# When the planner of an attention and GeGLU kernel may put zero products on TensorE

## The chip, the cores and the metric

One core of one Trainium2 chip runs the whole program. The metric is the device time of one execution in microseconds (us). The kernel before has a median of 792.99 us over five runs (791.52 to 793.93). The profile that is read below is of one execution of 792.45 us; its span from the first to the last instruction is 790.7 us, so 1.75 us of that execution lie outside the span.

## The reference

One transformer block on x of 2048 rows by 640 columns in bf16: 32 query heads of width 20 share one key head and one value head, and a gated MLP of width 1536 follows.

```python
h  = x + attention(layernorm(x))      # q = n @ wq, k = n @ wk, v = n @ wv, one k and v for 32 heads
                                      # softmax(q k^T / sqrt(20)) v, all heads side by side, then @ wo
h2 = h + (gelu(n2 @ w_gate) * (n2 @ w_up)) @ w_down      # n2 = layernorm(h)
```

## The kernel before

The rows are cut into 16 tiles of 128. Query rows are worked in nine chunks (seven of two tiles, two of one), and within a chunk in units of 512 query columns for each of four heads at a time. For a unit, each of the 16 key tiles gives a **pack** (`issue_qk`, L1092, product at L1149): four score tiles of 128 keys x 512 queries, computed side by side on four row groups of TensorE, each into a PSUM bank of its own (banks 0 to 5, sometimes 6 and 7).

A score tile is made into weights in one of two ways. ScalarE takes the exponential (L1489, one tile or a pair of neighbouring banks). Or VectorE makes a 16-bit approximation (`dve_decide`, L1583), of which GpSimd writes two shifted copies (L1552); such a tile costs three value products later, an exact one costs one. How many tiles of a pack go to VectorE (`n` in L1100 to L1111) follows from the load that the planner sees on both engines at that moment, from the free banks and from `stall`.

The value products (`issue_pv`, L1228) use four column groups of TensorE, one block of four products for the four row groups of heads, and add up in an accumulator bank (6 or 7) until the unit is closed and copied out (L1255). Projections, the MLP's products and the output projection go piecewise between them (`issue_piece`, all through the helper line L548). In this text a **block** is four products side by side on the four row or column groups.

The order of work on all five engines is not written by hand. A planner in Python (the loop at the end, L1698) walks forward in its own time: it takes the engine that is free first, asks that engine's `..._decide` for an instruction, and commits it with an estimated cost and latency; where there is nothing, the engine's time moves on by 20 ns. `plan.resolve` then sets the semaphore waits. Each engine's program is the order so found, and the hardware runs it in that order. Costs in the plan: 216 ns for a block of 512 columns, plus up to `SW` = 105 ns where the mode of TensorE changes between scores (`"q"`) and column-group work (`"v"`), in `pe_sw`.

`pe_decide` (L1271) issues a pack if four banks are free, else a value block, else a piece of another job. If none of these is to be had before the next pack is expected (`fits`, against `lim`), and if `quiet(t)` holds, `fill(t)` (L1342) issues a block of **zero products**: a weight of zeros (`zz`) against the first 512 columns of the keys, added to the accumulator of an open unit, which leaves the sum as it is. `quiet` adds up the planned time of TensorE in the last 3400 ns and compares it with `QUIET`. `fill` asks for a unit whose four row groups have started and with over 8 value products still to come (`u["todo"]`), and for the first four key tiles.

The start of the program (the head) loads x, computes the first layer norm tile by tile on VectorE, transposes the normed tiles by DMA on SyncE's queue (L487), and makes keys and values (`kv_job`) as tiles arrive, while the first packs already run. The four large weight loads (L983) come on the same SyncE queue behind a gate of planned time (L984):

```python
sp_tasks.append(_Task(("sp",), (lambda o, v: lambda e: e.dma_start(o[:], cview(v)))(o, v), 1500, 12000,
                      [], [nm], 9.0, None, lambda: plan.free["sp"] > 30000.0))
```

The second layer norm of a chunk (L423 to L496) is also VectorE work, and stands among the packs of a later chunk.

Of the kernel before, what the change touches and what calls it, by code (L numbers as in the profile page):

```python
# [9 lines left out]
P = 128  # L10
# [194 lines left out]
def bass_sequential_preLN__grouped_kv_mqa__glu_gated_geglu__prompt_kernel(  # L205
# [53 lines left out]
    def sb(name, shape, dt):  # L259
        cm = nc.sbuf_tensor(name, shape, dt)  # L260
        t = cm.__enter__()
        allocs.append(cm)
        return t
# [13 lines left out]
    kT4 = sb("kT4", [P, S], BF16)  # L277
# [12 lines left out]
    zz = sb("zz", [P, 32], BF16)  # L290
# [14 lines left out]
    ps = ps_cm.__enter__()  # L305
# [9 lines left out]
    plan = _Plan()  # L315
# [23 lines left out]
    SP2G = (300.0, 300.0, 300.0)  # L339
    ADD_MIN = 1  # L340
    PVF = 99
    QUIET = 0.5
    PADD_DVE = 1
    PADD_LEN = (3, 3, 3)
    PRA = 3
# [14 lines left out]
    L_PE, L_ACT, L_DVE, L_POOL = 232.0, 310.0, 150.0, 100.0  # L360
# [625 lines left out]
    def pe_sw(t, mode):  # L986

        if mode == state["mode"] or not plan.ops["pe"]:
            return 0.0
        return max(0.0, plan.ops["pe"][-1].end + SW - t)  # L990
# [6 lines left out]
    def open_units():  # L997
        return [u for u in units if u["npk"] > 0 and not u["evac"]]
# [272 lines left out]
    def pe_decide(t):  # L1271
# [58 lines left out]
        if fits(222.0 + swv) and quiet(t):  # L1330
            return fill(t)
        return False

    def quiet(t):
        busy = 0.0
        for o in reversed(plan.ops["pe"]):
            if o.end < t - 3400.0:
                break
            busy += min(o.end, t) - max(o.t0, t - 3400.0)
        return busy < QUIET * 3400.0  # L1340

    def fill(t):  # L1342

        u = next((u for u in open_units() if u["acc"] is not None and all(u["started"]) and u["todo"] > 8), None)
        if u is None or not all(("k", k) in plan.w and plan.ready("pe", [("k", k)], ()) <= t for k in range(4)):
            return False
        ab = u["acc"]

        def fn(e):
            ins = None  # L1350
            for r in range(4):
                ins = e.matmul(ps[32 * r:32 * r + 32, ab * 512:(ab + 1) * 512], zz[:], kT4[:, 0:512], start=False,
                               stop=False, tile_position=(0, 32 * r))
            return ins
        sw = pe_sw(t, "v")
        state["mode"] = "v"
        plan.commit("pe", fn, 216.0 + sw, L_PE, ["zz"] + [("k", k) for k in range(4)], [("b", ab)], at=t)
        state["fills"] = state.get("fills", 0) + 1
        return True

# [337 lines left out]
    while True:  # L1698
        eng = min(order, key=lambda e: plan.free[e])
        t = plan.free[eng]  # L1700
# [4 lines left out]
        if eng in ("pe", "dve", "act"):  # L1705
# [10 lines left out]
            k = (int(t // 100000), eng, why)  # L1716
# [23 lines left out]
    n = 0  # L1740
# [63 lines left out]
```

## Time and profile before

| what | value |
|---|---|
| median of five runs | 792.99 us (791.52 to 793.93) |
| the profiled execution, its span | 792.45 us, 790.7 us |
| mean granted TensorE clock | 0.976 |
| ScalarE busy, whole span; 60 to 765 us | 731.8 us; 686.2 of 705 us |
| TensorE busy | 698.2 us |
| VectorE and GpSimd busy | 613.9 and 655.4 us |
| zero products (L1352) | 148, that is 37 blocks, first at 33.9 us, last at 697.7 us |
| score tiles by ScalarE | 593 alone (653 ns each), 417 pairs (1078 ns each) |
| score tiles by VectorE | 621 (688 ns each) |

The rows are of the profile's page and its groups by line and shape. "PE" is TensorE, "ACT" ScalarE, "DVE" VectorE, "POOL" GpSimd, "SP" SyncE. A product's time in the profile includes the way through the array, so four products side by side show about 0.38 us busy when alone; in an unbroken run a block of 512 columns comes every 0.22 us.

### The profile page before, as it was taken

Reading aid. Unit: us, or ns where it says so; the run is one execution under the profiler, and the core shown is the slowest. Engines: PE = TensorE matmul, PEld = TensorE weight load, DVE = VectorE, ACT = ScalarE, POOL = GpSimd, SP = SyncE. Lnnn points to the kernel's source line nnn. Section 1 sums busy time; section 2 is a strip of 40 time slices with the busy share of each in tenths; the row PEclk is TensorE's granted clock in tenths of the full one; section 3 lists DMA queues with packets and bytes.
Section 4 is the critical chain, followed back from the end, with each engine's and each line's share of the span. In section 5 each row is a group of like instructions: output and inputs, shape, how many; then the busy total and the mean of one; then the engine's idle time right before and its main releaser. Section 6 shows DMA issues by size and latency. Waiting matters only on the chain.

```text
span 790.7 us, 29325 instructions
## 1 busy us (share of the span) xinstructions
PE 698.2 (88%) x12863; PEld 329.9 (42%) x12863; DVE 613.9 (78%) x1096; ACT 731.8 (93%) x1057; POOL 655.4 (83%) x708
## 2 busy tenths in 40 slices
PE   5668788888889899999889899999998989989998
PEld 3323223332234444445233444445543444434457
DVE  7948878888787877877787877868779787877854
ACT  5769999999999999999999999999999899999981
POOL 5569989999978997898987988789888898988860
PEclk9989999999989999999998999999999999989999
DMA  6790001100100012100010001200021001110000
GB/s 195 143 300 8 8 8 25 26 9 9 25 17 17 2 18 35 26 26 9 8 26 18 10 10 34 35 19 9 11 42 26 9 2 18 35 25 17 12 19 18
DMA packets 56606, 25.85 MB, mean 33 GB/s; under 512 B 47648, under 2 KB 55200, under 8 KB 56480
## 3 DMA queue, kind: packets, MB, share of 16 engines
q1 hardware_dynamic: 55168, 23.55, 13.3%
q8 instruction: 102, 1.67, 0.9%
q10 hardware_dynamic: 1312, 0.44, 0.3%
q14 instruction: 24, 0.20, 0.1%
HBM read 10.21 MB, written 2.62 MB: 16 GB/s over the span
## 4 chain that ended last, share of the span: by engine, by line
PE 57%; ACT 20%; DVE 15%; POOL 3%; DMA 3%; issue 2%; POOLq 0%
PE ps L548 21%; PE ps L1228 17%; ACT pa L1489 16%; PE ps L1149 16%; DVE pd L1583 10%; PE ps L544 3%; ACT gbuf L888 3%; POOL pd L1552 2%; DVE osb L1255 1%; DMA xn1T<-xn_tmp 1%; ACT L1489 1%; ACT L888 1%; DMA xh<-in_A_x_dram 1%; DVE xn_tmp L496 1%; DVE qT L618 1%
## 5 line engine op out<-in xcount | busy, mean ns | idle before, releaser
L1489 ACT ACTIVATE pa<-ps 128x512 bf16<-128x512 f32 (+1 forms) x1010 | 686.6, 829 | 31.3 <-PE ps L1149 25.3
L1552 POOL TENSOR_TENSOR pd<-pd,shifts 128x512 int32<-128x512 int32 x569 | 580.5, 1039 | 85.2 <-DVE pd L1583 80.1
L1583 DVE TENSOR_SCALAR pd<-ps 128x512 uint16<-128x512 f32 x621 | 416.4, 688 | 139.5 <-PE ps L1149 130.7
L1228 PE MATMUL ps<-pd,v_ext 128*32 128x512 bf16 x1863 | 292.2, 392 | 17.4 <-DVE osb L1255 10.1
L1228 PE MATMUL ps<-pa,v_ext 128*32 128x512 bf16 x1427 | 265.5, 394 | 3.1 <-DVE pd L1583 1.0
L1149 PE MATMUL ps<-qT,kT 32*128 32x512 bf16 x2048 | 206.6, 391 | 48.5 <-DVE pd L1583 30.0
L1149 PEld LDWEIGHTS ps<-qT,kT 32*128 32x128 bf16 x2048 | 57.0, 91 | 215.8 <-DVE pd L1583 130.6
L1228 PEld LDWEIGHTS ps<-pd,v_ext 128*32 128x32 bf16 x1863 | 80.1, 95 | 80.1 <-issue 37.1
L1228 PEld LDWEIGHTS ps<-pa,v_ext 128*32 128x32 bf16 x1427 | 71.1, 96 | 46.1 <-issue 26.7
L548 PE MATMUL ps<-xn2T,wu_sb 128*32 128x256 bf16 x1680 | 66.1, 274 | 2.8 <-DVE gbuf L905 1.7
L548 PE MATMUL ps<-xn2T,wg_sb 128*32 128x256 bf16 (+1 forms) x1748 | 67.9, 273 | 0.3 <-DVE gbuf L861 0.2
L548 PE MATMUL ps<-wd_sb,gbuf 128*32 128x320 bf16 x1344 | 65.3, 301 | 0.0
L548 PEld LDWEIGHTS ps<-xn2T,wg_sb 128*32 128x32 bf16 x1748 | 43.2, 97 | 19.7 <-issue 11.4
L548 PE MATMUL ps<-xn1T,wq_pad 128*32 128x256 bf16 (+1 forms) x1440 | 50.4, 266 | 0.8 <-POOL wq_pad L971 0.6
L548 PEld LDWEIGHTS ps<-xn2T,wu_sb 128*32 128x32 bf16 x1680 | 42.6, 96 | 19.7 <-issue 9.1
L548 PEld LDWEIGHTS ps<-wd_sb,gbuf 128*32 128x32 bf16 x1344 | 34.0, 96 | 24.2 <-issue 11.1
L548 PEld LDWEIGHTS ps<-xn1T,wq_pad 128*32 128x32 bf16 x1440 | 33.6, 97 | 14.1 <-issue 7.7
L905 DVE TENSOR_TENSOR gbuf<-ps,gbuf 128x512 bf16<-128x512 f32 x48 | 32.8, 682 | 8.5 <-PE ps L544 6.4
L1538 POOL TENSOR_TENSOR pd<-pd,shifts 128x256 int32<-128x256 int32 x50 | 33.4, 684 | 0.4 <-DVE pd L1583 0.4
L426 DVE BATCH_NORM_STATS2 stats<-xh 128x6 f32<-128x320 bf16 x64 | 30.0, 477 | 1.5 <-DMA xh<-in_A_x_dram 1.2
L548 PE MATMUL ps<-wo_sb,onT 128*32 128x320 bf16 x600 | 28.7, 301 | 1.5 <-DMA onT<-onq 1.1
L861 DVE CAST gbuf<-ps 128x512 bf16<-128x512 f32 x42 | 28.8, 685 | 0.9 <-PE ps L548 0.6
(73 smaller groups left out, 333.3 us busy)
## 6 DMA issues: line engine op xcount, KB each, us to landing
out_dram<-xh SPq DMA_DIRECT2D x16, 160.0 KB, 1.8
xh<-in_A_x_dram SPq DMA_DIRECT2D x3, 640.0 KB, 6.3
wg_sb<-in_B_w_gate_dram SPq DMA_DIRECT2D x1, 1920.0 KB, 10.9
wu_sb<-in_B_w_up_dram SPq DMA_DIRECT2D x1, 1920.0 KB, 10.8
wd_sb<-in_B_w_down_dram SPq DMA_DIRECT2D x1, 1920.0 KB, 15.4
wo_sb<-in_A_wo_dram SPq DMA_DIRECT2D x1, 800.0 KB, 5.1
onr<-osb SPq DMA_TRANSPOSE x30, 2.4
gbuf<-in_A_wq_dram ACTq DMA_DIRECT2D x1, 400.0 KB, 4.7
```

The lines of the kernel that those rows point to most:

```text
L426: dve(lambda e: e.bn_stats(stats[:, ln, t, 6 * h:6 * h + 6], xh[:, t, h * HALF:(h + 1) * HALF]), 395, [key], [("st", ln, t, h)], prio, c)
L544: return e.matmul(o(b), l, r, start=st, stop=sp)
L548: ins = e.matmul(o(b)[a, :], l[:, a], r, start=st, stop=sp, tile_position=(0, 32 * j))
L861: dve(lambda e: e.tensor_copy(o, i), c_dve(n * k), [("b", bk)], ks, 1.0, fin)
L888: task(("act",), (lambda v: lambda e: e.activation(v, v, ACT.Gelu_apprx_tanh))(v), ("gelu", c_act(n * (f1 - f0))), L_ACT, ks, ks, 1.0, (la ...
L905: dve(lambda e: e.tensor_tensor(o, i, o, ALU.mult), c_dve(n * k), [("b", bk)] + ks, ks, 1.0, fin)
L1149: ins = e.matmul(bank(b), kT4[32 * r:32 * r + 32, kt * P:(kt + 1) * P], qT[32 * r:32 * r + 32, s, :], start=True, stop=True, tile_position ...
L1228: ins = e.matmul(ps[32 * r:32 * r + 32, ab * 512:(ab + 1) * 512], v_ext[:, it["kt"], it["w"], :], it["ap"], start=st, stop=(j in ends), ti ...
L1489: op = plan.commit("act", lambda e: e.activation(dst, src, ACT.Exp, scale=SM_SCALE), cost, L_ACT, [("b", b0 + i) for i in range(n)], [("pa ...
L1538: return e.tensor_tensor(pd32[:, w, h], pd32[:, 0, h], shifts[:, w - 1:w].to_broadcast([P, 256 * k]), ALU.add)
L1552: return e.tensor_tensor(pd32[:, 1:3, h], pd32[:, 0, h].unsqueeze(1).to_broadcast([P, 2, 256]), shifts[:].unsqueeze(2).to_broadcast([P, 2, ...
L1583: op = plan.commit("dve", lambda e: e.tensor_scalar(pd[:, 0, s * 512:(s + 1) * 512], bank(b), CH_A, CH_B, ALU.mult, ALU.add), c_dve(512), ...
```

## The change

Five edits, all in the planner. `QUIET` goes from 0.5 to 0.55. `quiet` no longer counts an instruction's whole planned time but at most 213 ns at its end, which leaves out the mode change. `fill` asks for over `FTODO` = 4 value products still to come instead of over 8. Where the first four key tiles are not all there, two are enough, and the zero products are then 256 columns wide. The planned cost of a zero block becomes `n * P / 2.4 + 3.0`: 216.3 ns for four tiles in place of 216.0, 109.7 ns for two. Since every later decision of the planner sees the times that come out of this, the order of work after the first differing block can differ on all engines.

```diff
-    QUIET = 0.5
+    QUIET = 0.55
+    FTODO = 4
...
     def quiet(t):
+
         busy = 0.0
         for o in reversed(plan.ops["pe"]):
             if o.end < t - 3400.0:
                 break
-            busy += min(o.end, t) - max(o.t0, t - 3400.0)
+            busy += max(min(o.end, t) - max(o.end - min(o.end - o.t0, 213.0), t - 3400.0), 0.0)
         return busy < QUIET * 3400.0
 
     def fill(t):
 
-        u = next((u for u in open_units() if u["acc"] is not None and all(u["started"]) and u["todo"] > 8), None)
-        if u is None or not all(("k", k) in plan.w and plan.ready("pe", [("k", k)], ()) <= t for k in range(4)):
+        u = next((u for u in open_units() if u["acc"] is not None and all(u["started"]) and u["todo"] > FTODO), None)
+        n = 4 if all(("k", k) in plan.w and plan.ready("pe", [("k", k)], ()) <= t for k in range(4)) else 2
+        if u is None or not all(("k", k) in plan.w and plan.ready("pe", [("k", k)], ()) <= t for k in range(n)):
             return False
         ab = u["acc"]
 
         def fn(e):
             ins = None
             for r in range(4):
-                ins = e.matmul(ps[32 * r:32 * r + 32, ab * 512:(ab + 1) * 512], zz[:], kT4[:, 0:512], start=False,
+                ins = e.matmul(ps[32 * r:32 * r + 32, ab * 512:ab * 512 + n * P], zz[:], kT4[:, 0:n * P], start=False,
                                stop=False, tile_position=(0, 32 * r))
             return ins
         sw = pe_sw(t, "v")
         state["mode"] = "v"
-        plan.commit("pe", fn, 216.0 + sw, L_PE, ["zz"] + [("k", k) for k in range(4)], [("b", ab)], at=t)
+        plan.commit("pe", fn, n * P / 2.4 + 3.0 + sw, L_PE, ["zz"] + [("k", k) for k in range(n)], [("b", ab)], at=t)
```

## The prediction

> **What bounds the kernel now.** I read the page's busy line and slices first, then tables by stretch (60 to 765 us; then the 3.41 us steps in which the granted clock moves), then the chain around the clock's drops, and last the rows of the zero products. The busy line and the clock's slices:
>
> ```profile
> PE 698.2 (88%) x12863; PEld 329.9 (42%) x12863; DVE 613.9 (78%) x1096; ACT 731.8 (93%) x1057; POOL 655.4 (83%) x708
> ...
> PEclk9989999999989999999998999999999999989999
> ```
>
> ScalarE is the fullest engine. By stretch (us; busy us and instructions of PE, PEld, DVE, ACT, POOL; granted clock; DMA):
>
> ```profile
> 0.00:60.00 60.00, 36.95 (x670) 18.22 (x674) 42.18 (x127) 39.17 (x57) 34.95 (x67) 0.91 0.79 210
> 60.00:765.00 705.00, 638.45 (x11880) 292.09 (x11868) 561.36 (x948) 686.19 (x992) 618.88 (x640) 0.98 0.09 18
> ```
>
> From 60 to 765 us ScalarE idles for 705 - 686.2 = 18.8 us: no change of TensorE's order can win more there without giving ScalarE less to do. The head has 20.8 us of idle ScalarE more. The clock falls to half in eight places, 37.5 us in all. Below, three steps that came just before a drop, two after which the clock stayed whole, and four of the half-clock stretches:
>
> ```profile
> 97.17:100.59 3.42, 1.86 (x22) 0.51 (x22) 3.26 (x5) 3.39 (x7) 3.17 (x4) 1.00 0.00 0
> 418.03:421.44 3.41, 1.92 (x28) 0.55 (x24) 2.70 (x4) 3.27 (x5) 1.69 (x3) 1.00 0.17 34
> 609.17:612.59 3.42, 1.53 (x20) 0.57 (x20) 2.83 (x6) 2.67 (x5) 2.21 (x3) 1.00 0.50 96
> ...
> 28.91:32.32 3.41, 2.04 (x56) 0.97 (x55) 3.20 (x13) 2.21 (x4) 3.08 (x6) 1.00 0.77 77
> 394.13:397.55 3.42, 2.20 (x28) 0.72 (x24) 2.99 (x6) 3.42 (x7) 3.08 (x4) 1.00 0.02 5
> ```
>
> ```profile
> 100.59:104.00 3.41, 3.41 (x32) 0.77 (x28) 1.66 (x3) 2.15 (x4) 2.42 (x3) 0.50 0.41 43
> 230.29:237.12 6.83, 6.50 (x56) 1.26 (x52) 6.03 (x11) 5.75 (x8) 5.11 (x6) 0.50 0.15 26
> 421.44:424.85 3.41, 3.41 (x23) 0.60 (x23) 1.98 (x3) 2.08 (x5) 2.95 (x4) 0.50 0.24 48
> 612.59:616.00 3.41, 3.41 (x40) 1.20 (x43) 1.53 (x3) 2.35 (x4) 2.89 (x3) 0.50 0.02 5
> ```
>
> The reader is to see two things. A step with at most 1.92 us of busy TensorE was followed by half clock; of those I looked at, the emptiest that was not had 2.04 us. And in a half-clock stretch TensorE is full (3.41 of 3.41 us) while ScalarE, full before, idles: there TensorE is the bound.
>
> What comes ahead of a drop in mid-kernel is a layer norm's small work on VectorE, which frees score banks late. The chain at one of them (start, length, what):
>
> ```profile
> 228.31 1.03 DVE ln_veb L442
> 229.34 0.60 DVE pd L1583
> 229.94 0.14 issue
> 230.08 0.47 PE ps L1149 x4
> ...
> 232.02 0.97 PE ps L1228 x8
> 232.99 0.55 PE ps L1149 x3
> 233.54 0.97 PE ps L1228 x8
> 234.51 0.55 PE ps L1149 x4
> 235.06 0.55 PE ps L1352 x3
> ```
>
> TensorE had just been idle for 1.15 us waiting for L1583. The old rule placed no zero block there: its 3400 ns still held dense work, mode changes counted in.
>
> **The change, part by part.**
>
> *More zero blocks.* Counting 213 ns a block instead of 216 plus up to 105 lowers the counted load: with four changes in 3400 ns by about 0.42/3.4 = 0.12; the new bound adds 0.05. So the rule now asks for a real product share under 0.55 where it asked for about 0.35 to 0.5. In the timeline of TensorE I counted about 210 gaps of over 0.22 us, 116 us in all. Those with a share under 0.55 behind them hold about 137 blocks; the plan's gaps are not the trace's, so I take 100 new ones (60 to 140) beside the 37, most in the head, at 60 to 120, 180 to 230 and 380 to 425 us.
>
> *What a zero block costs.* It stands in a gap, so its own 0.22 us cost nothing while the gap is there. If the banks come free earlier than planned, the pack behind it, with ScalarE and VectorE behind that, is late by up to one block and a mode change: 0.21 us (its warm row on the chain, 114.20 us) to 0.33 (with a mode change as on the chain, 0.33 us a pack against 0.22 a block). Of the 37 blocks, five are on the chain, but four of these at half clock. Of some 31 at full clock, one: 0.21/31 = 0.007 us each, so 100 cost 0.7 us. Ends: 0, where every one is covered, and 100 x 0.33 x 1/4 = 8 us if every fourth hits. I take 0.7, by the nearest row, which is the same instruction.
>
> *The six drops in mid-kernel* (100.6, 230.3, 414.6, 421.4, 612.6 and 697.9 us, 27.3 us). ScalarE is busy there for 2.15 + 5.75 + 2.70 + 2.08 + 2.35 + 6.02 = 21.05 us, so it idles for 6.3. At full clock it wouldn't be full either: around the chunk end at 300 to 340 us, without any drop, it idles for 2.45 of 40 us, 6%, which is 1.6 us of 27.3. What can be won is 6.3 - 1.6 = 4.7 us. Five of the six need one more block in the step before (1.68 to 1.92 us of busy TensorE; a block alone shows 0.38), the one at 612.6 (1.53) about two. Each of these steps has a gap of 0.56 us or more, and its share at its end is low enough for the new rule. I take five sixths: -3.9 us. Ends: 0 and -4.7.
>
> *A rule against this.* The row: the gap of the drop at 230.3 us was 1.15 us, and none of the six had 3.4 us without a product. The Trainium skill ("TensorE: Matmul & The Clock Gate", "HAM oscillation — how this bites in real kernels") says that only a gap of over about 3.4 us must be avoided to keep the clock. By that rule alone one drop of eight, that behind the 5.3 us gap before 47.9 us, would be there, and this term would be 0 and the time 793.7. The rows speak against it.
>
> *The head.* Zero blocks 256 wide can now come before 33.9 us, while two key tiles exist. The step at 22.08 us had 1.35 us of busy TensorE, so it needs 0.6 us more, three to five narrow blocks. The todo bound lets them stand only between a pack and its value block, where gaps of 0.4 to 0.6 us lie at 23.5 and 25.3. If it works, the 2.32 us of key and value products at 25.88 us take half: 1.2 us. I take 0 of it, since the chain then goes through VectorE's layer norm and the 9.52 us at 38.28 in which a normed tile's transpose lands late behind the weight loads. The drop at 46 us, behind that wait, stays: the plan doesn't know the wait, and puts no block into it. Ends: 0 and -1.2.
>
> *The cost formula, 216.3 for 216.0 ns:* nothing that a 20 ns step shows. *No wait is added:* the keys are long there, and the last write of an accumulator stays a value block.
>
> *The order after it.* This the trace of before can't price. From both sides: two ends are the rivals below, +4.9 and -4.9 us by the load order, and +5 by the tiles' split. I take 0, as nothing in the rows gives a sign.
>
> Sum: 792.45 - 3.9 + 0.7 + 0 = 789.25 us against the profiled execution. The median of the runs shown lies 0.54 above it: 789.8 us, 0.4% faster.
>
> **The rivals.**
>
> *The blocks don't land where the drops are.* The planner counts 320 ns for the norm that took 596 (L496), 80 ns for steps that took 423 and 348 (L438, L442), so in its time those gaps are shorter than in the trace, and a zero block plus mode change needs 0.33 us. For it: no block was placed in five of the six steps before, though TensorE was at 1.5 to 1.9 of 3.4 us. Against it: three gaps of 0.56 us in the step at 609.17 alone. Then the drops stay and the blocks cost 0 to 1: 793 us (791 to 795).
>
> *Slower: more score tiles fall to ScalarE.* `n` is decided pack by pack from the loads at that instant (L1100 to L1111), and every instant after the first new block shifts. Price: 0.54 us of ScalarE for a tile in a pair (1078/2), 0.65 alone, on an engine 97% full. Ten tiles more of ScalarE's 593 + 2 x 417 = 1427 are 5.4 us. It decides from six tiles on: 6 x 0.54 = 3.2 us eats the net gain. With 13 tiles and the sum above: 789.8 + 7.0 = 797 us (793 to 800). For it: 1427 against 621 rests on thresholds. Against: the shift may go the other way as easily.
>
> *The load order in the head.* Two of the four weight loads left ahead of the last two transposes (L487 at 36.51 us). A load of 1920 KB at the 407 GB/s of 39 to 43 us is 4.8 us. One load more ahead: 789.8 + 4.8 = 795 us. One less: 785.
>
> **How the numbers follow.** About 0.2% (1.6 us) is what a measurement of this kernel can tell from no change. The forecast, 789.8 with 786 to 792, gets 0.44 (0.41 faster, 0.03 same): the rows of the drops are clear, but the gain is 4 us and the order moves. Blocks that don't land: 0.18 (0.04 faster, 0.08 same, 0.06 slower). Tiles to ScalarE: 0.27, slower. The load order: 0.11 (0.04 faster, 0.07 slower). Together: faster 0.49, same 0.11, slower 0.40. The range goes from 784.5 (one load less) to 800 (the upper end of the tiles); a fifth at most is left outside.
>
> **What would show it.** Right: L1352 with 400 to 700 products, some before 33.9 us; half-clock stretches of 10 to 20 us in all instead of 37.5, of which 6.8 at 46 us stay; ScalarE's idle time from 60 to 765 us at 14 to 16 us instead of 18.8. Wrong: as many drops as before (first rival), ScalarE's tiles over 1433 (second), three or more weight loads ahead of the last L487 (third), or many zero blocks on the chain at full clock (the cost term).

## The result, and the profile after

The changed kernel is slower: 795.64 us median (792.65 to 797.51) against 792.91 for the kernel before in the runs beside it, a ratio of 1.0036 with a 95% interval of 1.0026 to 1.0046. The forecast was 789.8 us. The profiled execution of the changed kernel has a span of 793.8 us. Its lines have moved by one to three: L1149 is now L1150, L1228 L1229, L1352 L1355, L1489 L1492, L1583 L1586, L487 L488, L983 L984, L725 L726.

The busy line and the clock's slices of the page after:

```profile
PE 705.3 (89%) x13176; PEld 334.9 (42%) x13176; DVE 617.1 (78%) x1106; ACT 729.3 (92%) x1060; POOL 659.0 (83%) x713
...
PEclk9979999999999999999999999999999999999999
```

The two stretches (us; busy us and instructions of PE, PEld, DVE, ACT, POOL; granted clock; DMA share; GB/s), and below them two steps of 3.4 us, each with the half-clock stretch that follows it:

```profile
0.00:60.00 60.00, 34.16 (x650) 17.00 (x654) 38.15 (x122) 35.38 (x52) 31.83 (x64) 0.92 0.79 210
60.00:765.00 705.00, 645.21 (x12136) 296.63 (x12128) 566.95 (x961) 684.78 (x996) 622.74 (x645) 1.00 0.09 18
```

```profile
47.53:50.94 3.41, 0.00 (x0) 0.00 (x0) 0.00 (x0) 0.08 (x1) 0.15 (x1) 1.00 1.43 279
50.94:61.18 10.24, 7.14 (x73) 2.16 (x73) 3.20 (x6) 3.97 (x6) 4.51 (x6) 0.50 0.68 214
231.87:235.28 3.41, 1.77 (x24) 0.59 (x28) 3.38 (x7) 2.70 (x6) 2.54 (x4) 1.00 0.21 43
235.28:238.70 3.42, 3.42 (x32) 0.76 (x24) 2.22 (x6) 2.66 (x4) 2.37 (x4) 0.50 0.24 48
```

Two things are to be seen. From 60 to 765 us the clock is whole but for one step of 3.4 us, behind a step with 1.77 us of busy TensorE; the six drops of mid-kernel have become one. And the head has got worse: ScalarE works 35.4 of the first 60 us instead of 39.2, nothing at all runs on TensorE from 47.5 to 50.9 us, and 10.2 us at half clock follow instead of 6.8.

The head's wait is on SyncE's queue. What that queue issued (start, length, engine, line, kind), first before, then after:

```profile
34.37 0.59 SPq L983 DMA_DIRECT2D wo_sb<-in_A_wo_dram  x1
35.01 0.52 SPq L983 DMA_DIRECT2D wg_sb<-in_B_w_gate_dram  x1
36.51 5.48 SPq L487 DMA_TRANSPOSE xn1T<-xn_tmp  x2
42.04 0.77 SPq L983 DMA_DIRECT2D wu_sb<-in_B_w_up_dram  x1
```

```profile
35.38 0.58 SPq L984 DMA_DIRECT2D wo_sb<-in_A_wo_dram  x1
36.01 0.52 SPq L984 DMA_DIRECT2D wg_sb<-in_B_w_gate_dram  x1
36.57 0.53 SPq L984 DMA_DIRECT2D wu_sb<-in_B_w_up_dram  x1
37.84 10.86 SPq L488 DMA_TRANSPOSE xn1T<-xn_tmp  x2
```

The third weight load now goes out ahead of the last two transposes of the first layer norm, and these take 10.86 us on the queue instead of 5.48. The chain says the same: it waits for that transpose until 47.80 us before and until 53.16 after. Before, then after:

```profile
38.28 9.52 DMA xn1T<-xn_tmp
```

```profile
45.32 7.84 DMA xn1T<-xn_tmp
53.16 0.09 issue
53.25 1.26 PE ps L549 x15
```

The zero products, before and after, in the groups by line and shape:

```profile
L1352 PE MATMUL ps<-kT,zz 128*32 128x512 bf16 x148 | 14.9, 415 | 0.0
```

```profile
L1355 PE MATMUL ps<-kT,zz 128*32 128x512 bf16 x456 | 41.5, 396 | 0.0
```

114 blocks instead of 37, the first at 24.3 us, and none of them 256 wide: wherever the planner placed one, four key tiles were there.

### The profile page after: what moved, and what is told of

It is laid out like the page before. It is cut to its first block, busy times and chain, and to the rows that moved or that the text cites. A ratio compares the mean times of both kernels' runs of the same rounds, so it can differ in the third digit from the quotient of the medians.

```text
span 793.8 us, 29951 instructions
## 1 busy us (share of the span) xinstructions
PE 705.3 (89%) x13176; PEld 334.9 (42%) x13176; DVE 617.1 (78%) x1106; ACT 729.3 (92%) x1060; POOL 659.0 (83%) x713
## 4 chain that ended last, share of the span: by engine, by line
PE 59%; ACT 16%; DVE 16%; DMA 6%; issue 1%; POOL 1%
PE ps L549 22%; PE ps L1229 17%; PE ps L1150 16%; ACT pa L1492 14%; DVE pd L1586 9%; PE ps L545 3%; DMA onr<-osb 3%; DMA xn1T<-xn_tmp 2%; ACT gbuf L889 2%; DVE osb L1256 1%; PE ps L1355 1%; DVE xn_tmp L497 1%; DMA xh<-in_A_x_dram 1%; POOL pd L1555 1%; DVE qT L619 1%
## 5 line engine op out<-in xcount | busy, mean ns | idle before, releaser
L1492 ACT ACTIVATE pa<-ps 128x512 bf16<-128x512 f32 (+1 forms) x1011 | 683.4, 821 | 37.0 <-PE ps L1150 31.0
L1586 DVE TENSOR_SCALAR pd<-ps 128x512 uint16<-128x512 f32 x628 | 420.0, 688 | 130.1 <-PE ps L1150 120.5
L1229 PE MATMUL ps<-pd,v_ext 128*32 128x512 bf16 x1884 | 292.2, 385 | 17.8 <-DVE osb L1256 12.9
L1229 PE MATMUL ps<-pa,v_ext 128*32 128x512 bf16 x1420 | 257.0, 386 | 4.7 <-ACT pa L1492 2.3
L1150 PE MATMUL ps<-qT,kT 32*128 32x512 bf16 x2048 | 203.3, 385 | 37.5 <-DVE pd L1586 18.3
L1150 PEld LDWEIGHTS ps<-qT,kT 32*128 32x128 bf16 x2048 | 56.3, 91 | 204.3 <-DVE pd L1586 130.2
L1229 PEld LDWEIGHTS ps<-pd,v_ext 128*32 128x32 bf16 x1884 | 80.2, 95 | 77.5 <-issue 30.4
L1229 PEld LDWEIGHTS ps<-pa,v_ext 128*32 128x32 bf16 x1420 | 69.7, 95 | 45.0 <-issue 25.0
L1355 PE MATMUL ps<-kT,zz 128*32 128x512 bf16 x456 | 41.5, 396 | 0.0
L1541 POOL TENSOR_TENSOR pd<-pd,shifts 128x256 int32<-128x256 int32 x54 | 35.5, 674 | 0.6 <-DVE pd L1586 0.6
```

What stands on the lines that cost most here:

```text
L1150: ins = e.matmul(bank(b), kT4[32 * r:32 * r + 32, kt * P:(kt + 1) * P], qT[32 * r:32 * r + 32, s, :], start=True, stop=True, tile_position ...
L1355: ins = e.matmul(ps[32 * r:32 * r + 32, ab * 512:ab * 512 + n * P], zz[:], kT4[:, 0:n * P], start=False, stop=False, tile_position=(0, 32 ...
L1492: op = plan.commit("act", lambda e: e.activation(dst, src, ACT.Exp, scale=SM_SCALE), cost, L_ACT, [("b", b0 + i) for i in range(n)], [("pa ...
L1541: return e.tensor_tensor(pd32[:, w, h], pd32[:, 0, h], shifts[:, w - 1:w].to_broadcast([P, 256 * k]), ALU.add)
L1586: op = plan.commit("dve", lambda e: e.tensor_scalar(pd[:, 0, s * 512:(s + 1) * 512], bank(b), CH_A, CH_B, ALU.mult, ALU.add), c_dve(512), ...
```

## The experiments

Two theories stood against each other at first. A: the load order costs 4 to 5 us, and the rest of the change wins 1 to 2. B: the load order is nearly hidden, and the zero blocks on the chain cost the 3 us. A ratio is always that to the kernel before, measured again beside the runs in question. No edit touches the planner's decisions: each changes the finished order or what a zero block issues, so that every instruction not named stays in its place. In the first four, DMA issues are moved on SyncE's queue just before `plan.resolve()`.

**1. The changed kernel with the load order of before.**

```diff
+    spq = plan.ops["sp"]
+    late = [plan.w["wu"][0]]
+    for op in late:
+        spq.remove(op)
+    at = 1 + max(spq.index(plan.w[("xn1T", t)][0]) for t in range(2, NT))
+    spq[at:at] = late
     plan.resolve()
```

> The changed kernel with every engine's order as it is, except that on SyncE's queue the third weight load (w_up) goes behind the last two transposes of the first layer norm, as in the kernel before. Theory A, the load order: the 1920 KB ahead of those transposes cost 4 to 5 us of the changed kernel's 795.6, and the zero blocks and the rest of the new order won 1 to 2 us. Then this runs at 791 to 792 us, ratio to the kernel before 0.997 to 0.999. Theory B, the zero blocks on the chain: the load order is nearly hidden by ScalarE's slack later, and the zero blocks cost about 3 us net. Then this runs at 794.5 to 796, ratio 1.002 to 1.004.

Measured: 789.03 us, ratio 0.9953 (0.9928 to 0.9978). The one load, put back, moves the changed kernel from 1.0036 to 0.9953, 0.83% or 6.6 us (4.4 to 8.7 with both intervals). This is theory A, and faster than the 791 to 792 us that it gave. The chain now waits for the last transpose until 48.53 us, 4.6 us less:

```profile
43.17 5.36 DMA xn1T<-xn_tmp
```

**2. The kernel before with the load order of after.**

```diff
+    spq = plan.ops["sp"]
+    op = plan.w["wu"][0]
+    spq.remove(op)
+    spq.insert(1 + spq.index(plan.w["wg"][0]), op)
     plan.resolve()
```

> The kernel before with every engine's order as it is, except that the w_up load goes ahead of the last two transposes of the first layer norm, as in the changed kernel. Theory A: slower by 4 to 5 us, 797 to 798 us, ratio 1.005 to 1.006, and ScalarE busy in the first 60 us falls from 39.2 to about 35 us. Theory B: 793 to 794 us, ratio 1.000 to 1.001.

Measured: 796.76 us, ratio 1.0058 (1.0038 to 1.0077), 4.6 us slower (3.0 to 6.1); ScalarE works 35.0 of the first 60 us. The chain waits for the last transpose until 51.93 us, 4.1 us more than before:

```profile
44.10 7.83 DMA xn1T<-xn_tmp
```

The same move of one DMA issue makes either kernel slower, by 4.6 and by 6.6 us. Theory B falls.

Which edit of the change moved the load? The order that the planner writes for SyncE's queue with each edit alone shows it (the number of weight loads ahead of the last two transposes):

```
edit alone                         loads ahead
213 ns counted in quiet                 3
QUIET 0.55                              3
todo bound 4                            2
cost formula of the zero block          2
```

Either of the first two is enough. They change no cost of a load; they shift the order in the planner's own time at the moments, after 30 us of it, when SyncE asks what to send next.

**3 and 4. All four loads behind the last two transposes**, in both kernels: the edit of run 1 with `late = [plan.w[k][0] for k in ("wo", "wg", "wu", "wd")]`.

> The changed kernel with all four large weight loads behind the last two transposes of the first layer norm on SyncE's queue; all else in its order. Theory A: three loads of 4640 KB in all leave the wait in the head, so over 8 us go from it if nothing else is late next; what is next is VectorE's layer norm, so 6 to 8 us: 788 to 790 us, ratio 0.994 to 0.996. Theory B: 794 to 795 us.

> The kernel before with all four large weight loads behind the last two transposes of the first layer norm; all else in its order. Theory A: the wait of 5 to 6 us on those transposes goes, and with it the half-clock stretch at 46 us: 787 to 789 us, ratio 0.992 to 0.995. Beside the third kernel it gives the worth of the zero blocks and the new order without the head's wait: by theory A the changed kernel is the faster of these two by 1 to 2 us, by theory B the slower by 3. Theory B: 792 to 793.

Measured: 793.97 us, ratio 1.0010 (0.9996 to 1.0025), and 792.75 us, ratio 1.0003 (0.9987 to 1.0018). Theory A missed in both. The times are near those that theory B gave (794 to 795, and 792 to 793), but the 3 us that it put between the two kernels aren't there, and its reason isn't what the chain shows. The wait for the last transposes of the layer norm had gone, and another came in its place: the loads now stood ahead of the first unit's transpose of outputs. The chain's wait for it, the changed kernel first, the kernel before second:

```profile
55.54 9.62 DMA onr<-osb
```

```profile
54.61 8.35 DMA onr<-osb
```

ScalarE works 51.8 and 53.2 us from 60 to 120 us, against 58.2 in both kernels as they were. A queue's load has to stand somewhere; the gain was given back one wait later.

**5 and 6. No zero blocks.** Run 5 takes the changed kernel with the load order of before, run 6 the kernel before. `zero` is the list of what `fill` committed.

```diff
+    out_of = set(map(id, zero))
+    plan.ops["pe"] = [op for op in plan.ops["pe"] if id(op) not in out_of]
+    for i, op in enumerate(plan.ops["pe"]):
+        op.idx = i
     plan.resolve()
```

> The changed kernel with the load order of the kernel before (789.0 us), and all 114 blocks of zero products left out as the program is written; every other instruction stays in its place. Theory A1, the clock: the zero blocks won the 3.4 us against the kernel before; without them the clock falls in more places than the eight of the kernel before, and this runs at 793 to 797 us, ratio 1.000 to 1.006. Theory A2, the split: the 3.4 us came from the seven score tiles fewer on ScalarE (1420 instead of 1427, 0.54 us each, 3.8 us), and the zero blocks pay only for themselves; then this runs at 788 to 790 us, ratio 0.994 to 0.997, whatever the clock shows.

> The kernel before without its 37 blocks of zero products; every other instruction stays in its place. Theory A1: more drops of the clock, 794 to 797 us, ratio 1.002 to 1.006. Theory A2: 791.5 to 793 us, ratio 0.999 to 1.001.

Measured: 795.27 us, ratio 1.0040 (1.0018 to 1.0061), with 58.0 us at half clock ahead of the end; and 795.83 us, ratio 1.0055 (1.0035 to 1.0075), with 47.8 us. So the 114 blocks of the changed kernel are worth 1.0040 - 0.9953 = 0.87%, 6.9 us, and the 37 of the kernel before 0.55%, 4.4 us. Both runs go as theory A1 has it. Without any block the two orders are equal within their intervals, although ScalarE has 1420 score tiles in one and 1427 in the other: no worth of the split shows, and the 788 to 790 us that A2 gave for run 5 are far off.

**7. Zero blocks half as wide**, on the order of run 1: `ab * 512:ab * 512 + 2 * P` and `kT4[:, 0:2 * P]` in `fill`'s product.

> The changed kernel with the load order of the kernel before (789.0 us), its 114 blocks of zero products 256 columns wide instead of 512, all in their places. If what a zero block costs is the time in which a pack stands behind it (some 10 us of zero blocks lie on the changed kernel's chain), half of that comes back where the clock holds: 786 to 788 us, ratio 0.992 to 0.994. If half a block is too little to hold the clock, the drops come back and it runs at 790 to 793 us.

Measured: 789.31 us, ratio 0.9968 (0.9950 to 0.9987); 17.1 us at half clock, against 6.8 in run 1. The time lies between the two that were expected, with no gain over run 1 (0.9953) and no loss beyond the intervals: inconclusive on the price of a block.

**8. The loads spread.** w_o and w_gate behind the last two transposes, w_up behind the first unit's transpose of outputs, w_down behind the second's.

```diff
+    spq = plan.ops["sp"]
+    loads = [plan.w[k][0] for k in ("wo", "wg", "wu", "wd")]
+    for op in loads:
+        spq.remove(op)
+    at = 1 + max(spq.index(plan.w[("xn1T", t)][0]) for t in range(2, NT))
+    spq[at + 2:at + 2] = loads[3:]
+    spq[at + 1:at + 1] = loads[2:3]
+    spq[at:at] = loads[:2]
     plan.resolve()
```

> The changed kernel with the loads spread on SyncE's queue: w_o and w_gate behind the last two transposes of the first layer norm, w_up behind the first unit's transpose of outputs, w_down behind the second's. With all loads behind the last two transposes, that first unit's transpose waited 8 to 10 us, which ate the gain; here nothing should stand before it. Theory A: the wait of 5.4 us that the changed kernel with the order of before still had at 43 us goes, and nothing takes its place: 784 to 786 us, ratio 0.989 to 0.992. If the two loads ahead still hold the unit's transpose, 788 to 791.

Measured: 786.90 us, ratio 0.9939 (0.9913 to 0.9965), a little above the 784 to 786 of theory A. The queue now runs without a long transpose (the longest of these two kinds takes 2.8 us), and from 36 to 72 us the chain waits for none:

```profile
44.61 0.58 SPq L984 DMA_DIRECT2D wo_sb<-in_A_wo_dram  x1
45.24 0.52 SPq L984 DMA_DIRECT2D wg_sb<-in_B_w_gate_dram  x1
56.84 1.19 SPq L726 DMA_TRANSPOSE onr<-osb  x1
58.08 0.58 SPq L984 DMA_DIRECT2D wu_sb<-in_B_w_up_dram  x1
```

**9. The same in the kernel before.**

> The kernel before with the loads spread on SyncE's queue as in the run at 786.9 us (w_o and w_gate behind the last two transposes of the first layer norm, w_up and w_down behind the first and second unit's transposes of outputs); all else in its order. It stands beside that run as the kernel before beside the changed one, without a load in anybody's way. Theory A1, the clock: the 77 blocks more are worth 2.5 to 3.5 us there too, so 789 to 790.5 us, ratio 0.996 to 0.998. If the gain of spreading the loads depends on the changed order, 791 to 793 us.

Measured: 785.62 us, ratio 0.9923 (0.9899 to 0.9946). Theory A1 asked for 0.996 to 0.998 and missed: without a load in the way, the kernel before is as fast as the changed one.

**10 and 11. Which zero blocks pay, loads spread.** The edit of run 5 with the list cut at 50 us of planned time: first without the 17 blocks of the head, then with them alone.

> The changed kernel with the loads spread (786.9 us), without the 17 blocks of zero products of the first 52 us; the other 97 stay. Theory A1: the head has several drops without them, among them the long one that the order without any zero block showed at 31.6 us (17.1 us), but the head also waits for VectorE and for loads; 0.5 to 2.5 us slower than with them, 787.5 to 789.5 us, ratio 0.994 to 0.997. If the head's blocks are worth nothing: 786 to 787.5.

> The changed kernel with the loads spread (786.9 us), with only the 17 blocks of zero products of the first 52 us; the 97 later ones are left out. Theory A1: the drops of the middle come back, some ten of them; 4 to 6 us slower than with them, 790.5 to 793 us, ratio 0.998 to 1.001. If the later blocks pay only for themselves: 786 to 788.

Measured: 787.93 us, ratio 0.9939 (0.9917 to 0.9961), and 788.65 us, ratio 0.9954 (0.9937 to 0.9971). Both intervals overlap that of run 8 (0.9913 to 0.9965): beside it, neither group shows a worth of its own. Run 15 below comes back to this.

**12. Each zero block issued twice**, loads spread: `for r in (0, 1, 2, 3, 0, 1, 2, 3):` in `fill`.

> The changed kernel with the loads spread (786.9 us), each of its 114 blocks of zero products issued twice in its place, 114 blocks more. The clock is whole already, so this measures what a block costs. By the prediction's term, 0.007 us each: 0.8 us more, 787.7 us, ratio 0.995. By the blocks on the changed kernel's chain, some 10 us for 114: up to 10 us more, 792 to 797 us, ratio 1.000 to 1.006. Every fourth hit at 0.33 us, the prediction's upper end: 9 us.

Measured: 795.96 us, ratio 1.0057 (1.0037 to 1.0077). Against the 0.9939 and 0.9917 of the two runs without the doubling this is 1.18 to 1.40%, 9 to 11 us for 114 blocks, 0.08 to 0.10 us each, near the upper ends of the forecast. The chain's shares by line, run 8 and then this one (the list goes on to the right):

```profile
by line: PE ps L549 22.0%; PE ps L1229 16.1%; ACT pa L1492 15.6%; PE ps L1150 15.5%; DVE pd L1586 8.7%; PE ps L545 2.7%; ACT gbuf L889 2.2%; DMA onr<-osb 2.1%; issue 1.5%; DVE osb L1256 1.4%; PE ps L1355 1.2%; DVE xn_tmp L497 1.1%; POOL pd 
```

```profile
by line: PE ps L549 21.6%; PE ps L1229 18.6%; PE ps L1150 17.3%; DVE pd L1586 9.3%; ACT pa L1492 8.9%; PE ps L1355 5.0%; PE ps L545 2.6%; ACT gbuf L889 1.8%; DMA onr<-osb 1.6%; DVE osb L1256 1.6%; issue 1.6%; DVE xn_tmp L497 1.1%; DVE stats
```

The zero products (L1355) go from 1.2% to 5.0% of the chain, and ScalarE's exponentials from 15.6% to 8.9%: more blocks stand on the chain, and ScalarE, which waits for packs, idles for 22.9 us between the 64th and the last pack in place of 16.9. That fits second blocks that find no room in the gaps.

**13 to 16. Head or mid-kernel.** Left open was where run 1 had its gain, since runs 8 and 9 showed none. Theory H: in the head, where the blocks take away the half clock behind the wait. Theory M: in mid-kernel, as predicted. The edits are those of runs 10 and 11 on the load order of before, and runs 8 and 9 again, side by side on one chip.

> The changed kernel with the load order of the kernel before (789.0 us), without the 17 blocks of zero products of the first 52 us; the other 97 stay. Theory H, the head: the gain of 3.4 us comes from the head's blocks, which keep the clock behind the wait for the loads; without them 791 to 793 us, ratio 0.998 to 1.001. Theory M, mid-kernel as predicted: the gain comes from the later blocks and stays; 789 to 790 us, ratio 0.995 to 0.997.

> The changed kernel with the load order of the kernel before (789.0 us), with only the 17 blocks of zero products of the first 52 us. Theory H: the later blocks pay about for themselves, so 789 to 791 us, ratio 0.996 to 0.998. Theory M: 792 to 795 us, ratio 1.000 to 1.004.

> The changed kernel with the loads spread on SyncE's queue, once more, on the same chip as the next. Theory H: with the wait gone there is nothing in the head to win, and the later blocks cost what they save: equal to the next within 1 us, both at 785 to 787 us. Theory M: faster than the next by 2.5 to 3.5 us.

> The kernel before with the loads spread on SyncE's queue, once more, on the same chip as the run before it. Theory H: 785 to 787 us, equal to it within 1 us. Theory M: slower than it by 2.5 to 3.5 us.

Measured: without the head's blocks 789.56 us, ratio 0.9966 (0.9950 to 0.9982); with them alone 792.51 us, 0.9993 (0.9974 to 1.0012). Most of the gain on the load order of before comes with the later blocks, as M has it. With the loads spread: 785.77 us, 0.9917 (0.9897 to 0.9938), and 786.66 us, 0.9925 (0.9901 to 0.9949): equal, as H has it. So neither holds alone. Run 15 is the kernel of run 8 once more, and beside it run 11, without the later blocks (0.9954, 0.9937 to 0.9971), is slower by 0.37% with intervals that barely touch: a worth of the later blocks with the loads spread is not shown, but not excluded either.

The traces give the place, one execution each, by the start of the 64th and of the last pack (us):

```
                                 64th pack   last pack   between
before                             114.7       763.2      648.5
after, load order of before        111.7       759.4      647.7
before, load order of after        118.8       765.0      646.2
after                              118.7       765.7      647.0
before, all loads behind           115.4       763.8      648.4
after, all loads behind            117.4       761.8      644.4
before, loads spread (two)     109.7, 110.0  757.1, 755.8  647.4, 645.8
after, loads spread (two)      111.3, 111.0  756.5, 756.2  645.2, 645.2
```

At the same load order the changed kernel is ahead between the two packs by 0.8 us where two loads stand before the transposes, by 0.6 to 2.2 with the loads spread and by 4.0 with all four behind; with three loads ahead it is behind by 0.8. Two executions of one kernel differ there by 1.6. Up to the 64th pack it is 3.0 us ahead with two loads before the transposes, level with three, and 1.0 to 2.0 behind where none stands there: in run 8 the last transpose of the layer norm goes out at 43.4 us, in run 9 at 38.9. In the whole time the change is clear of noise only with two loads ahead, 0.47% faster. With three the ratios are 1.0036 and 1.0058, with all four behind 1.0010 and 1.0003, and with the loads spread they are equal, all with overlapping intervals. So what the zero blocks of the change are worth depends on the load order, and how the small gain divides stays open.

## Why the prediction was wrong

The step that failed is *the order after it*, which was set to 0. The third rival had the mechanism, the place and nearly the time: one load more ahead of the last two transposes, +4.8 us, 795 us. It had a chance of 0.07 as a slower case. What the kernel's text did show was that SyncE's queue sends loads wherever it finds nothing else after 30 us of planned time, between transposes of tiles that VectorE delivers just then; a small shift can cross a boundary of that kind, and two of the change's edits do so alone, so it deserved more than a tenth. The mechanism is shown from both sides (runs 1 and 2): one load moved is 6.6 us in the changed kernel and 4.6 in the kernel before, where the sum had 0.

The rival's price of 4.8 us is about what the last transpose is late by: 4.6 us in the changed kernel (53.16 us against 48.53 in run 1) and 4.1 in the kernel before (51.93 in run 2 against 47.80). Whether the 6.6 us of the whole time is really more than the 4.6 isn't settled, since their intervals overlap. The traces have one thing that goes that way: behind the wait the changed kernel has 10.2 us at half clock, and none in run 1, while the kernel before has 6.8 us there and 10.2 with the moved load.

*The drops in mid-kernel* (-3.9 us): the blocks landed and six drops became one, so the first rival falls, and the rule on steps held: the one drop left followed a step with 1.77 us, under the 1.92. The sum without the load, 789.8 us, stands beside 789.0 in run 1. But that is probably partly luck, as the next paragraph tells, and it holds for this load order alone: with the loads spread the same blocks show no gain (runs 8, 9, 15 and 16), which the term didn't foresee.

*What a zero block costs* was mis-sized by about ten: 0.007 us taken, 0.08 to 0.10 measured for a second block in the same place. For the first in its place that is more likely a bound from above, as the gap is emptier then; no run measures it. The nearest row, one warm block of 31 on the chain, was a poor one: on the chain of the changed kernel zero products make up 1.3% of 793.8 us, about 10 us, where the prediction had 0.7, though time on the chain isn't yet time lost. Runs 5 and 6 show only what the blocks are worth with their cost taken off: 4.4 us for the 37 old ones, 6.9 for all 114, so about 2.5 for the 77 new ones. If the new ones cost near 0.09 us each, 7 us in all, they must have won more than the 4.7 us that the prediction took to be there, and two errors stood against each other; no run separates the two.

*The reading of ScalarE's idle time* failed: 14 to 16 us was forecast for 60 to 765 us, and it is 20.2 after and 22.5 in run 1, which is faster. Some 2 us of the 22.5 come from the fixed stretch, as run 1 has its last pack before 760 us; between the 64th and the last pack ScalarE idles for 17.1 us before, 18.5 after and 19.2 in run 1. Two things stand behind it. ScalarE has less to do, 729.3 us in place of 731.8: nine tiles alone more and eight pairs fewer are -2.7 us at 0.653 and 1.078. And the new order has small waits in stretches that had been full: from 380 to 400 us it works 19.1 us where it had worked 19.8, from 180 to 222 us 40.7 where it had worked 41.7. Run 5, without any zero block, has 19.0 and 40.8 there, which speaks for the order as the cause and not for the blocks.

*The number of blocks* (100 new, 60 to 140) was 77. The count behind it was too high: 116 us of gaps are more than the 790.7 - 698.2 = 92.5 us in which TensorE idles at all by the busy line. *The narrow blocks*, taken as 0, were 0, since none was placed. *More tiles to ScalarE*, the second rival: they went the other way, to 1420, and runs 5 and 6 show no worth of it.

*The rule weighed* (the Trainium skill, "TensorE: Matmul & The Clock Gate", "HAM oscillation — how this bites in real kernels") reads "no PE-idle gaps >~3.4µs". Keeping to it is again not enough here: the step ahead of the drop at 235.28 us had 1.77 us of busy TensorE, so at most 1.64 us of gap. That shorter gaps are harmless, as the prediction read it, the sentence doesn't say.

## What to carry to other kernels

A planner that sends large loads on a queue "when nothing else is ready" can put them ahead of short transfers on which everything waits, and a small change elsewhere may move one across: compare the order of each DMA queue before reading anything else out of two traces. Such loads are placed by what comes behind them: all of them behind one critical transfer only held up the next, while spreading them, two behind the last transposes of the layer norm and one behind each of the next two transposes, gave the fastest versions here, 785.6 to 786.9 us, with either zero-block rule (ratios 0.9917 to 0.9939). Idle products that hold the clock were worth 4.4 and 6.9 us here on the load order of before, and where they weren't needed a second one cost about a tenth of a microsecond; the 77 that the change adds showed a gain clear of noise on one load order of four.

## What the runs showed of the hardware

In the two kernels the granted clock went to half behind steps of 3.4 us with 1.92 us or less of busy TensorE, and not behind those looked at with more (1.93 us in the changed kernel at 562.93 us, 2.04 in the kernel before). Busy time is no sharp boundary, though: run 1 kept its clock behind a step with 1.86 us (555.48 to 558.89 us), and run 11 lost it behind one with 2.13 (412.82 to 416.24 us). In mid-kernel no step ahead of a drop in the two kernels was idle for more than 1.9 us in all (1.53 us busy of 3.41). Products with a weight of zeros held the clock: without the 37 blocks the time at half clock rose from 37.5 to 47.8 us, and without the 114, on the load order of before, from 6.8 to 58.0 us. And the last two transposes of 128 x 640, behind 4640 KB of loads on the same queue, took SyncE 10.86 us, behind 2720 KB 5.48 us; the median of the fourteen transposes is 1.28 us each.
